# Strassen-Winograd pairs in a fused attention and GEGLU kernel: more pairs, two at a time

## The chip, the cores and the metric

One core of one Trainium2 chip runs the whole program. The metric is the device time of one launch in microseconds. A core has five engines with a queue each: PE (TensorE, matrix products, with PEld for its weight loads), DVE (VectorE), ACT (ScalarE), POOL (GpSimd) and SP, which issues transfers. PE writes only to PSUM, eight banks of 128 x 512 float32; the other engines empty those banks into SBUF, except POOL, which works on SBUF alone here.

## The reference

```
q' = exp(q - max) / sum over the head's 64 columns
k' = exp(k - max) / sum over the 576 rows
x  = q' @ (k'^T @ v)              # per batch (8) and head (8); heads side by side: 4608 x 512
h  = gelu(x @ w_gate) * (x @ w_val)   # 512 -> 1536, twice
out = h @ w_out                       # 1536 -> 512, float32
```

## The kernel before

**Blocks.** The 576 rows of a batch are cut into 512 main rows and 64 remaining ones. The main rows of batch b are block b (0 to 7). The remaining rows of all eight batches, 8 x 64 = 512, are gathered in `xtr` and make block 8. The order is 0, 1, ..., 6, 8, 7. Every block goes through two parts: the *gate/value part* makes `ht`, 12 chunks of 128 rows of h (transposed: 128 hidden columns by 512 rows of x), and the *output part* multiplies it by w_out.

**The direct way.** For one chunk and one of gate and value, four matmuls of 128x128 by 128x512 (one per 128 columns of x). ACT takes the gelu of the gate bank to SBUF, DVE multiplies it with the value bank and writes `ht`. Each such half-chunk is a call of `half`.

**Pairs.** From block 3 on, some chunks are made two at a time by the Strassen-Winograd scheme: chunks k and k+3 with both halves of the 512 rows form a 2x2 block product that takes seven products of half size instead of eight (`product_gv`, L572). A pair has four steps in `fi_pairs`: products 1 and 5 (with an ACT copy of bank pa to pb, L623, and a snapshot of pc, L608); 6 and 3; 7 and 2; 4. It holds three banks, pa, pb and pc. The results for the upper 256 rows are assembled by DVE in a float32 tile `cc` (L612), go through a gelu on ACT (L639), and are multiplied to `ht` by POOL (L640). The lower 256 rows come from pb and pa by an ACT gelu and a DVE product (L601, L602). The scheme needs sums of weight blocks, made once by `sum_wgv` on DVE, and four sums of x per block, made by `sum_x` on POOL (L570) from the finished `xt`. In blocks 3 to 8, six of the twelve chunks are pairs (k = 0, 1, 2) and six are direct.

**Output.** From block 1 on, `out_strassen` (L668) does the same with h: seven products of twelve 128x256 matmuls, accumulated in banks a, b and c, with snapshots `sn` (L690) and additions `yo` (L696) on DVE between them. It needs sums of h blocks: `sum_h` (L552) makes `sh` on DVE and, for most columns, the other two on POOL. A snapshot of a bank must be finished before the next product adds to that bank.

**What sets the order.** Everything is written out by hand: each engine executes its instructions in the order in which the Python code emits them. Small jobs for the attention of later batches are hung on points of that order by `at(b, kind, i, ...)` and emitted by `ride(b, kind, i)`. They are: loads, `exp` on ACT, the norm of q (`norm_sum` on DVE, `norm_mul` on POOL), the transposing transfer `unit_td`, the cast of v on POOL (`cast_v`), the k'^T v product `unit_kv4` and the x product `unit_x4`. Banks are handed out by `big`: the tag that was free longest goes next, and a held bank returns at `let_go`.

Of the kernel before, what the change touches and what calls it, by code (L numbers as in the profile page):

```python
# [18 lines left out]
def kernel(  # L19
# [86 lines left out]
    for i in range(2):  # L106
# [6 lines left out]
    ws = {nm: const.tile([P, 3, 2, NO // 2 * P], f16, name=f"ws{nm}") for nm in "gv"}  # L113
    xs = const.tile([P, 4, 2, 256], f16)
    q0r = const.tile([64, H, D], f32)
    eq0r = const.tile([P, C], f16)
    ld_b = {nm: [const.tile([P, H, NC * D], f32, name=f"{nm}t{i}") for i in range(n)]
            for nm, n in (("k", 2), ("v", 1), ("q", 1))}

# [29 lines left out]
    def load(src, nm, b, h0, h1, n0):  # L149
        tiles[(nm, b)] = ld_b[nm][b % len(ld_b[nm])]  # L150
        for t, c0 in ((0, n0), (1, 1)):
            (nc.scalar if b == 0 and t == 1 else nc.sync).dma_start(
                out=tiles[(nm, b)][t:P:2, h0:h1, c0 * D:NC * D],
                in_=src[b, h0:h1].rearrange("h (m n) d -> m h (n d)", n=NT)[
                    :, :, (4 * t + c0) * D:(4 * t + NC) * D])
# [36 lines left out]
    def exp(nm, b, h0=0, h1=H, n0=0):  # L192
        dst = ek_b[0] if nm == "k" else eq_b[b % 2]
        o, i = (("p n (c t d) -> p c t n d", "p c t (n d) -> p c t n d") if b >= QUAD else
                ("p n (h d) -> p h n d", "p h (n d) -> p h n d"))
        nc.scalar.activation(  # L196
            out=dst[:, n0:NC, h0 * D:h1 * D].rearrange(o, d=D, **({"t": 2} if b >= QUAD else {})),
            in_=heads(tiles[(nm, b)], b, h0, h1)[..., n0 * D:NC * D].rearrange(i, d=D),
            func=ACTF.Exp)
# [10 lines left out]
    def norm_sum(b, hp, n0=0):  # L210
        n = NC - n0
        e = eq_b[b % 2][:, n0:NC, hp * P:(hp + 1) * P].rearrange("p n (h d) -> p n h d", d=D)
        rq = att.tile([P, n, 2], f32, name="rq", tag="rq", bufs=4)
        nc.vector.reduce_sum(rq, e, axis=mybir.AxisListType.X)  # L214
        rrq = att.tile([P, n, 2], f32, name="rrq", tag="rrq", bufs=4)
        nc.vector.reciprocal(out=rrq, in_=rq)
        st[(b, "norm", hp)] = (e, rrq, n)

    def norm_pair(b, g, n0, engs):

        n = NC - n0
        e = eq_b[b % 2][:, n0:NC, 2 * g * P:(2 * g + 2) * P].rearrange("p n (h d) -> p n h d", d=D)
        rq = att.tile([P, n, 4], f32, name="rq2", tag="rq2", bufs=2)
        nc.vector.reduce_sum(rq, e, axis=mybir.AxisListType.X)
        rrq = att.tile([P, n, 4], f32, name="rrq2", tag="rrq2", bufs=2)
        nc.vector.reciprocal(out=rrq, in_=rq)  # L226
        for j, eng in enumerate(engs):
            st[(b, "norm", 2 * g + j)] = (e[:, :, 2 * j:2 * j + 2], rrq[:, :, 2 * j:2 * j + 2], n)
            norm_mul(b, 2 * g + j, eng)
# [9 lines left out]

    def exp_rem0():  # L240
        nc.scalar.activation(out=eq0r[0:64, :].rearrange("p (h d) -> p h d", d=D), in_=q0r,
                             func=ACTF.Exp)

    def norm_rem0():
# [5 lines left out]
        nc.vector.tensor_tensor(  # L250
# [84 lines left out]
    def unit_t(b, g, eng="dve", between=()):  # L335
# [3 lines left out]
        for j in range(2):  # L339
            hp = 2 * g + j  # L340
            for f in between if j == 1 else ():
                f()
            for n in range(NM):
                nc.tensor.transpose(
                    pst[:, j, n * P:(n + 1) * P],
                    eq_b[b % 2][:, n + 1, hp * P:(hp + 1) * P], ident)
# [3 lines left out]
    def unit_trem(b):  # L350

        src = eq0r[0:64] if b == 0 else eq_b[b % 2][:, 0, :]
# [6 lines left out]
    def unit_td(b):  # L359
# [3 lines left out]
                                    in_=eq_b[b % 2].rearrange("p n c -> p (n c)"))  # L363
# [192 lines left out]
    def sum_wgv(nm, i):  # L556
        w = wg_sb if nm == "g" else wv_sb
        n = NO // 2 * P
        a11, a21 = w[:, 0:2, 0:n], w[:, 0:2, n:2 * n]
        a12, a22 = w[:, 2:4, 0:n], w[:, 2:4, n:2 * n]  # L560
        t = [ws[nm][:, i] for i in range(3)]
# [4 lines left out]
    def sum_x(xt):  # L566
# [5 lines left out]
    def product_gv(i, ps, xt, k, first):  # L572
        lo, hi = slice(k * P, (k + 1) * P), slice((k + NO // 2) * P, (k + NO // 2 + 1) * P)
        for t, w, nm in ((0, wv_sb, "v"), (1, wg_sb, "g")):
            for c in range(2):
                a = {1: w[:, c, lo], 2: w[:, 2 + c, lo], 3: ws[nm][:, 2, c, lo], 4: w[:, 2 + c, hi],
                     5: ws[nm][:, 0, c, lo], 6: ws[nm][:, 1, c, lo], 7: w[:, c, hi]}[i]
# [5 lines left out]
    def fi_pairs(b, xt):  # L583
        cs = [(c, nm) for k in range(NO // 2) for c in (NO + k, NO + NO // 2 + k) for nm in "gv"]
        psg = {}

        def half(n):
            c, nm = cs[n]
            t = big([P, 512], f32, "ps" + nm)
            mm_gv(t, wg_sb if nm == "g" else wv_sb, xt, c, range(HP))  # L590
            if nm == "g":
                psg[c] = ffn.tile([P, 512], f32, name="gl", tag="gl")
                nc.scalar.activation(out=psg[c], in_=t, func=ACTF.Gelu)  # L593
            else:
                nc.vector.scalar_tensor_tensor(out=ht[:, c, :], in0=t, scalar=_H_SCALE,  # L595
                                               in1=psg[c], op0=ALU.mult, op1=ALU.mult)
            ride(b, HF, n)

        def final(ps, fi):
# [6 lines left out]
        def snap(ps):  # L606
            sn = ffn.tile([P, 2, 256], f32, name="snq", tag="snq", bufs=3)
# [6 lines left out]

        ride(b, HF, -1)
        half(0)
        half(1)
        for k in range(NO // 2):
            cc = ffn.tile([P, 2, 2, 256], f32, name="cc", tag="cc", bufs=1)
# [6 lines left out]
            s5 = snap(pc)  # L626
            half(3 * k + 2)
# [5 lines left out]
            half(3 * k + 3)  # L633
# [4 lines left out]
            glc = ffn.tile([P, 2, 256], f32, name="glc", tag="gl")  # L638
            nc.scalar.activation(out=glc, in_=cc[:, :, 1], func=ACTF.Gelu, scale=1.0 / _H_SCALE)  # L639
            nc.gpsimd.tensor_tensor(  # L640
                out=ht[:, k:NO:NO // 2, 256:512], in0=cc[:, :, 0], in1=glc, op=ALU.mult)
            half(3 * k + 4)
            product_gv(4, pa, xt, k, False)
            final(pa, k + NO // 2)
            if k == NO // 2 - 1:
                half(11)
            ride(b, PR, k)
# [3 lines left out]
    def product(i, ps, first, ts=(0, 1)):  # L651
        for j in range(NO):
            for t in ts:
# [5 lines left out]
                if w is None:  # L659
                    w = tw[{4: 4, 5: 1, 6: 2, 7: 3}[i]][:, j]  # L660
                nc.tensor.matmul(ps[t], a, w, start=(first and j == 0 and (  # L661
                    t == ts[0] or ps[t].tensor is not ps[ts[0]].tensor)),
                                 stop=(j == NO - 1), skip_group_check=True)
# [4 lines left out]
    def out_strassen(b, last):  # L668
# [31 lines left out]
        def second():  # L700
            get("b")
            product(2, ps["b"], True)
            add("b", s1, 0, 0)
            for x in tiles_["b"]:
                let_go(x)

        late = b == B
        get("a")
        product(1, ps["a"], True)
        s1 = snap("a")  # L710
        if not late:
            second()
        sum_h(*last_js(b), (4,))
        get("c")
        product(5, ps["c"], True)
        if not late:
            sum_h(*last_js(b), (3,))
        s5 = snap("c")
        if late:
            sum_h(*last_js(b), (3,))  # L720
        product(6, ps["a"], False)
        s2 = snap("a")
        ride(b, NS, 2)
        product(3, ps["c"], False)
        add("c", s2, 0, 1)
        for x in tiles_["c"]:
            let_go(x)
        if not late:
            store_rows(b, 0, yo[0])
# [3 lines left out]
        product(7, ps["a"], False)  # L733
        add("a", s5, 1, 1)
        ride(b, NS, 4)
        if late:
            second()
            store_rows(b, 0, yo[0])
        product(4, ps["a"], False)
# [101 lines left out]
    FI, NS, HF, PR = range(4)  # L841
# [7 lines left out]
    def load_2nd():  # L849
        load_batch(2, ((q, "q"), (k, "k")))  # L850
        for h0 in (0, 4):
            nc.sync.dma_start(out=q0r[:, h0:h0 + 4], in_=q[0, h0:h0 + 4].rearrange(
                "h (m n) d -> m h (n d)", n=NT)[:, :, 0:D])
# [42 lines left out]
    at(2, FI, NFI - 1, L(exp, "q", 4), L(exp, "k", 4), exp_rem0)  # L896
    at(3, HF, 8, L(norm_rem0))
    at(3, HF, 11, L(unit_trem, 0))
    for b in range(3, B):
        n = b + 1  # L900
        if n < B:
            at(b, HF, -1, L(norm_sum, n, 0), L(norm_mul, n, 0, "pool"), L(norm_sum, n, 1),
               L(norm_mul, n, 1, "pool"))
            at(b, HF, 1, L(norm_sum, n, 2), L(norm_mul, n, 2, "pool"))
            at(b, HF, 2, L(norm_sum, n, 3), L(norm_mul, n, 3, "pool"))
            at(b, HF, 3, L(unit_td, n))
        if n + 1 < B:
            at(b, HF, 0, L(load_2, n + 1))
            at(b, HF, 5, L(cast_v, n + 1, 0, 4))
            at(b, HF, 8, L(cast_v, n + 1, 4, 8))  # L910
            at(b, HF, 11, L(exp, "q", n + 1), L(exp, "k", n + 1))
    for b in range(2, B - 1):
        n = b + 1
        at(b, NS, 4, L(unit_x4, n, ("act", "dve"), 0 if n == 4 else None))
# [4 lines left out]
        at(b, NS, 4, L(preload, ACTF.Gelu), L(lambda n: sum_x(get_xt(n)), n) if n < B - 1 else L(sum_x, xtr))  # L919
    at(B, NS, 2, L(lambda: sum_x(get_xt(B - 1))))  # L920
    for b in range(3, B + 1):
        for j in range(NO // 2 - 1):
            at(b, PR, j, L(sum_h, j, NO, (1, 2)), L(sum_h, j, NO, (3, 4), "pool"))
# [6 lines left out]
    for b in order:  # L930
# [9 lines left out]
        if b > 2:  # L940
            fi_pairs(b, xt)
# [18 lines left out]
        else:  # L960
            sum_h(*last_js(b), (1, 2))
# [31 lines left out]
```

## Time and profile before

The median is 301.44 us (three runs, 301.3 to 301.6); the profiled execution spans 299.4 us.

| engine | busy us | share of the span |
|---|---|---|
| PE | 287.1 | 96% |
| DVE | 213.5 | 71% |
| ACT | 173.1 | 58% |
| POOL | 161.7 | 54% |

| groups that the change touches | count | mean ns |
|---|---|---|
| direct matmuls of gate, value 128x512 (L443) | 264 each | 379 |
| matmuls of pairs 128x256 (L580) | 504 | 273 |
| DVE `cc` (L612), 128x512 | 36 | 684 |
| POOL product to `ht` (L640), 128x512 | 18 | 1267 |
| POOL sums of x (L570), 128x512 | 24 | 1190 |
| POOL cast of v (L172), 128x640 | 26 | 769 |
| POOL norm of q (L233), 128x640 | 25 | 1282 |

[...]Matmuls overlap, so the price of one is the distance from its start to the next one's. The same holds, in a smaller measure, for ACT and DVE: the next instruction starts before the one ahead has ended. A share of the span is a mean over stages; a stage has to be read by itself.

### The profile page before, as it was taken

What the parts mean: (1) busy time and instruction counts of PE and PEld (TensorE: products, weight loads), DVE (VectorE), ACT (ScalarE), POOL (GpSimd) and SP (SyncE); (2) the same over time, 40 slices, a digit from 0 to 9 for tenths busy, and PEclk for the clock granted to TensorE, in tenths of its full rate; (3) what the DMA queues carried; (4) which work ended last, traced back from release to release, by engine and by line L of the source; (5) the groups of instructions that cost most, each with busy time, mean ns of one, the idle gap of its engine ahead of it and who ended that gap; (6) DMA issues with size and microseconds to landing.
All of it is one profiled execution on the core that took longest, in us unless ns stands there. A gap on an engine that the chain in (4) does not pass through costs nothing. (4 is left out here: it accounts for less than half of the span.)

```text
span 299.4 us, 5905 instructions
## 1 busy us (share of the span) xinstructions
PE 287.1 (96%) x2293; PEld 188.4 (63%) x2293; DVE 213.5 (71%) x411; ACT 173.1 (58%) x269; POOL 161.7 (54%) x149
## 2 busy tenths in 40 slices
PE   3999999999999999899999999999999999899994
PEld 1544445446744586568666876687668666676683
DVE  2953479998767889786867786878687557845762
ACT  4763467777652576558656956595652465126530
POOL 1557558870336009991599359944981536803610
PEclk9999999999999999999999999999999999999999
DMA  7999999997189106960399029802140300023003
GB/s 225 372 383 390 400 389 388 332 319 208 74 286 306 42 2 227 384 100 2 127 344 233 3 113 347 242 2 101 54 77 0 123 21 0 2 61 81 0 2 140
DMA packets 54619, 51.69 MB, mean 173 GB/s; under 512 B 18496, under 2 KB 50496, under 8 KB 54592
## 3 DMA queue, kind: packets, MB, share of 16 engines
q1 hardware_dynamic: 52864, 49.49, 52.0%
q10 hardware_dynamic: 1728, 1.84, 1.9%
q8 instruction: 18, 0.29, 0.4%
q14 instruction: 9, 0.07, 0.1%
HBM read 37.75 MB, written 9.44 MB: 158 GB/s over the span
## 5 line engine op out<-in xcount | busy, mean ns | idle before, releaser
L443 PE MATMUL psg<-xt,wg_sb 128*128 128x512 f16 x264 | 69.8, 379 | 0.0
L443 PE MATMUL psv<-xt,wv_sb 128*128 128x512 f16 x264 | 69.7, 379 | 0.0
L443 PEld LDWEIGHTS <-wv_sb 128*128 128x128 f16 x288 | 28.1, 98 | 27.4 <-issue 0.2
L233 POOL TENSOR_TENSOR eq<-eq,rrq 128x640 f16<-128x640 f16 (+1 forms) x27 | 34.5, 1297 | 19.7 <-DVE rrq L226 7.3
L443 PEld LDWEIGHTS <-wg_sb 128*128 128x128 f16 x288 | 28.1, 98 | 25.3
L661 PEld LDWEIGHTS <-ht 128*128 128x128 f16 x384 | 37.2, 98 | 7.1 <-issue 0.8
L448 ACT ACTIVATE gl<-psg 128x512 f32<-128x512 f32 x36 | 21.0, 597 | 29.0 <-PE psg L443 28.9
L640 POOL TENSOR_TENSOR ht<-cc,glc 128x512 f16<-128x512 f32 x18 | 22.8, 1267 | 24.1 <-ACT glc L639 24.1
L449 DVE SCALAR_TENSOR_TENSOR ht<-psv,gl 128x512 f16<-128x512 f32 x36 | 24.2, 684 | 16.0 <-PE psv L443 13.7
L570 POOL TENSOR_TENSOR xs<-xt 128x512 f16<-128x512 f16 x10 | 12.0, 1200 | 43.1 <-ACT xt L174 43.1
L595 DVE SCALAR_TENSOR_TENSOR ht<-psv,gl 128x512 f16<-128x512 f32 x36 | 24.6, 684 | 4.5 <-PE psv L443 2.4
L593 ACT ACTIVATE gl<-psg 128x512 f32<-128x512 f32 x36 | 21.3, 591 | 7.9 <-PE psg L443 7.8
L172 POOL CAST v<-vt 128x640 f16<-128x640 f32 x26 | 19.1, 769 | 12.0 <-PE pskv L319 10.5
L661 PE MATMUL psa<-tw,ht 128*128 128x256 f16 x192 | 23.5, 273 | 0.2 <-DVE yo L696 0.2
L214 DVE TENSOR_REDUCE rq<-eq 128x10 f32<-128x640 f16 x28 | 22.2, 793 | 1.6 <-ACT eq L196 1.6
L196 ACT ACTIVATE ek<-kt 128x1280 f16<-128x1280 f32 (+1 forms) x11 | 19.1, 1748 | 5.6 <-DMA kt<-in_k_dram 4.1
L580 PEld LDWEIGHTS <-wv_sb 128*128 128x128 f16 x144 | 14.0, 98 | 12.8 <-DVE cc L612 1.8
L661 PEld LDWEIGHTS <-sh 128*128 128x128 f16 x192 | 18.7, 98 | 3.5 <-issue 1.0
L552 POOL TENSOR_TENSOR ht<-ht 128x512 f16<-128x512 f16 x12 | 16.7, 1396 | 6.5 <-DVE sh L552 6.5
L196 ACT ACTIVATE eq<-qt 128x2560 f16<-128x2560 f32 (+2 forms) x10 | 18.4, 1863 | 2.6 <-DMA qt<-in_q_dram 2.5
L601 ACT ACTIVATE glq<-pgb 128x256 f32<-128x256 f32 x18 | 6.9, 383 | 21.6 <-PE pgb L580 21.2
L612 DVE SCALAR_TENSOR_TENSOR cc<-pgc,snq 128x512 f32<-128x512 f32 x18 | 12.4, 686 | 7.5 <-ACT snq L608 7.5
(136 smaller groups left out, 566.5 us busy)
## 6 DMA issues: line engine op xcount, KB each, us to landing
out_dram<-yo SPq DMA_DIRECT2D x15, 512.0 KB, 3.4
kt<-in_k_dram SPq DMA_DIRECT2D x7, 640.0 KB, 8.4
vt<-in_v_dram SPq DMA_DIRECT2D x7, 640.0 KB, 5.1
qt<-in_q_dram SPq DMA_DIRECT2D x7, 640.0 KB, 6.8
qt<-in_q_dram SPq DMA_DIRECT2D x8, 512.0 KB, 7.4
wost<-in_moe_w_out_dram SPq DMA_DIRECT2D x6, 512.0 KB, 7.9
kt<-in_k_dram SPq DMA_DIRECT2D x6, 512.0 KB, 9.8
vt<-in_v_dram SPq DMA_DIRECT2D x6, 512.0 KB, 5.7
```

The lines of the kernel that those rows point to most:

```text
L172: nc.gpsimd.tensor_copy(out=dst, in_=src)
L196: nc.scalar.activation(out=dst[:, n0:NC, h0 * D:h1 * D].rearrange(o, d=D, **({"t": 2} if b >= QUAD else {})), in_=heads(tiles[(nm, b)], b, ...
L214: nc.vector.reduce_sum(rq, e, axis=mybir.AxisListType.X)
L233: (nc.gpsimd if eng == "pool" else nc.vector).tensor_tensor(out=e, in0=e, in1=rrq.unsqueeze(-1).to_broadcast((P, n, 2, D)), op=ALU.mult)
L443: nc.tensor.matmul(ps, w[:, ci, fi * P:(fi + 1) * P], xt[:, ci, :], start=(ci == 0), stop=(ci == HP - 1))
L448: nc.scalar.activation(out=gl, in_=psg, func=ACTF.Gelu)
L449: nc.vector.scalar_tensor_tensor(out=ht[:, fi, :], in0=psv, scalar=_H_SCALE, in1=gl, op0=ALU.mult, op1=ALU.mult)
L552: (nc.gpsimd if eng == "pool" else nc.vector).tensor_tensor(out=o, in0=a, in1=b, op=op)
L593: nc.scalar.activation(out=psg[c], in_=t, func=ACTF.Gelu)
L595: nc.vector.scalar_tensor_tensor(out=ht[:, c, :], in0=t, scalar=_H_SCALE, in1=psg[c], op0=ALU.mult, op1=ALU.mult)
L640: nc.gpsimd.tensor_tensor(out=ht[:, k:NO:NO // 2, 256:512], in0=cc[:, :, 0], in1=glc, op=ALU.mult)
L661: nc.tensor.matmul(ps[t], a, w, start=(first and j == 0 and (t == ts[0] or ps[t].tensor is not ps[ts[0]].tensor)), stop=(j == NO - 1), ski ...
```

## The change

**More pairs.** Blocks 4 to 6 make four pairs (k = 0, 1, 2 and 6, the last being chunks 6 and 9), blocks 8 and 7 make six (k = 0, 1, 2, 6, 7, 8), so that these two have no direct chunk. The purpose is one eighth fewer matmul columns per pair. The weight sums for the new pairs are made by DVE in the output parts of blocks 3 to 6. Room for them is taken from the second k tile (`kt1`); a second `cc` and the second set of sums of x lie in the second eq tile and in the v tile, so blocks from 4 on use one buffer each of k and eq.

**Two pairs in turns.** The order of a gate/value part is now a string of steps (`THREE`, `FOUR`, `SIX`): "0.1" is step 1 of pair 0, "7g" is the gate of direct chunk 7, a bare word is a point for small jobs. Two pairs alternate, so that ACT and DVE have time between two steps of the same pair. The two alternate between two `cc` tiles, and the gelu writes into `cc` in place.

**The output takes late tiles late.** The first output product runs over chunks 0, 3, 1, 4 first; step 4 of the last pair ("2.4", or "8.4" in blocks 8 and 7) is emitted between those and the rest, with the second product in between in blocks 4 to 6. In block 8's output, step 1 of block 7's first pair stands ahead of the last product.

**Small jobs moved.** The cast of v goes from the gate/value part into the output part. The norm sums of q take two head pairs at once. The remaining rows of batch 0 are loaded, normalized and multiplied later (blocks 4 to 6 instead of 0 to 3), and their last norm product is on POOL. The sums of x for block 7 go from block 8's output to point `s0` of its gate/value part. The upper product of the very last pair of blocks 8 and 7 is made by DVE.

```diff
-    def fi_pairs(b, xt):
-        cs = [(c, nm) for k in range(NO // 2) for c in (NO + k, NO + NO // 2 + k) for nm in "gv"]
...
+    THREE = ("a 6g l 6v n 0.1 9g 0.2 9v t 0.3 7g 0.4 s0 1.1 7v 1.2 10g 1.3 10v 1.4 s1 2.1 8g 2.2"
+             " 8v 2.3 11g 2.4 11v")
+    FOUR = ("a 7g l 7v n 0.1 6.1 0.2 6.2 t 0.3 6.3 10g 0.4 6.4 s0 1.1 10v 1.2 8g 1.3 8v 1.4 s1 2.1"
+            " 11g 2.2 11v 2.3")
+    SIX = ("0.1 6.1 0.2 6.2 0.3 6.3 0.4 1.1 6.4 s0 7.1 1.2 7.2 1.3 7.3 1.4 2.1 7.4 s1 8.1 2.2 8.2"
+           " 2.3 8.3 2.4")
+    steps = {b: (THREE if b == 3 else SIX if b >= B - 1 else FOUR).split() for b in range(3, B + 1)}
...
+        def upper(cc):
+            nc.scalar.activation(out=cc[:, :, 1], in_=cc[:, :, 1], func=ACTF.Gelu,
+                                 scale=1.0 / _H_SCALE)
+            (nc.vector if k == NFI - NO // 2 - 1 else nc.gpsimd).tensor_tensor(
+                out=ht[:, k:k + NO // 2 + 1:NO // 2, 256:512], in0=cc[:, :, 0], in1=cc[:, :, 1],
+                op=ALU.mult)
...
+        js = (0, 1, 2, 3, 4, 5) if b < 3 else (0, 3, 1, 4, 2, 5)
         get("a")
-        product(1, ps["a"], True)
+        product(1, ps["a"], True, js=js[:4])
+        if b > 3:
+            pair_step(b, get_x(b), NO // 2 - 1 if b < B - 1 else NFI - NO // 2 - 1, 4)
+        ride(b, PR, "e")
+        get("b")
+        if 3 < b < B - 1:
+            product(2, ps["b"], True, js=js)
+        product(1, ps["a"], False, js=js[4:])
+        sum_h(*last_js(b), (1, 2))
         s1 = snap("a")
...
+        if b == B:
+            go_on(B - 1, get_x(B - 1), 1)
+        product(4, ps["a"], False, js=js)
...
-            at(b, HF, 5, L(cast_v, n + 1, 0, 4))
-            at(b, HF, 8, L(cast_v, n + 1, 4, 8))
-            at(b, HF, 11, L(exp, "q", n + 1), L(exp, "k", n + 1))
+            at(b, PR, "l", L(load_2, n + 1))
+            at(b, NS, 2, L(cast_v, n + 1, 0, H))
+            at(b, PR, "e", L(exp, "q", n + 1), L(exp, "k", n + 1))
...
-    at(B, NS, 2, L(lambda: sum_x(get_xt(B - 1))))
+    at(B, PR, "s0", L(lambda: sum_x(get_x(B - 1), xs_b[1])))
     for b in range(3, B + 1):
         for j in range(NO // 2 - 1):
-            at(b, PR, j, L(sum_h, j, NO, (1, 2)), L(sum_h, j, NO, (3, 4), "pool"))
+            at(b, PR, f"s{j}", L(sum_h, j, NO, (1, 2)), L(sum_h, j, NO, (3, 4), "pool"))
+    for b, i, what in ((3, 1, "g1 v1"), (3, 2, "g2 v2 g3 v3"), (3, 3, "g4 v4")):
+        for x in what.split():
+            at(b, NS, i, L(sum_wgv, x[0], int(x[1]), NO, 1))
+    for b, i, what in ((4, 2, "g1 g2"), (4, 3, "g4"), (5, 2, "v1 v2"), (6, 1, "v4"),
+                       (6, 2, "g3 v3")):
+        for x in what.split():
+            at(b, NS, i, L(sum_wgv, x[0], int(x[1]), NO + 1, 2))
```

## The prediction

> **What bounds the kernel now.** I read the table of stages first (one row per block's gate/value part and per block's output part; cut points from the timeline of TensorE), then TensorE's waits, then the chain that ended last, then one stretch of the timeline.
>
> The stages (stretch, us, then busy time of PE, PEld, DVE, ACT, POOL, granted clock, DMA share, GB/s):
>
> ```profile
> 113.87:135.51 21.64, 19.87 (x135) 12.83 (x132) 17.53 (x34) 12.78 (x27) 20.11 (x19) 1.00 0.76 222
> 135.51:146.28 10.77, 10.77 (x149) 9.18 (x148) 8.53 (x17) 8.31 (x9) 1.50 (x2) 1.00 0.13 50
> 146.28:165.85 19.57, 19.57 (x135) 12.90 (x132) 14.37 (x30) 13.01 (x27) 18.41 (x18) 1.00 0.86 242
> 165.85:176.73 10.88, 10.81 (x141) 9.04 (x140) 8.37 (x18) 8.26 (x8) 2.53 (x3) 1.00 0.13 50
> ...
> 236.55:256.08 19.53, 19.53 (x134) 12.91 (x132) 11.07 (x22) 12.55 (x25) 11.45 (x10) 1.00 0.07 29
> 256.08:266.43 10.35, 9.51 (x86) 8.13 (x85) 8.27 (x12) 0.00 (x0) 5.37 (x5) 1.00 0.01 2
> 266.43:285.96 19.53, 19.53 (x135) 12.92 (x133) 11.05 (x21) 12.54 (x25) 8.37 (x7) 1.00 0.24 55
> ```
>
> Rows 1 and 2 are block 3, rows 3 and 4 block 4, then block 8 (two rows) and block 7. TensorE is busy wall to wall in nearly all; the second number to see is POOL: 18.4 to 20.1 us of 19.6 to 21.6 in blocks 3 and 4, and almost idle in the output part behind them.
>
> TensorE's waits (us in total, times, longest):
>
> ```profile
> PE pswarm L435 <- ACT warm L787: 4.9, 1, 4.9
> PE pga L580 <- DVE cc L612: 1.8, 2, 1.4
> PE psa L661 <- DVE sn L690: 0.8, 1, 0.8
> ```
>
> Past the start TensorE waits for VectorE alone: in block 3 for `cc`, in block 8's output for `sn`. Against an unstalled 19.53, block 3 loses 2.11 us; block 8's output takes 10.35 where its seven products need 7 x 1.31 = 9.17, so it loses 1.18.
>
> Prices of TensorE, from the chain that ended last (start, us, what):
>
> ```profile
> 263.97 1.31 PE psb L661 x12
> ...
> 267.45 0.86 PE psv L443 x4
> 268.32 0.44 PE pga L580 x4
> ```
>
> Why block 8's output stalls (timeline: start, us, engine, line, what):
>
> ```profile
> 256.50 1.15 POOL L570 TENSOR_TENSOR xs<-xt 128x512 f16<-128x512 f16 x1
> 257.11 0.82 DVE L552 TENSOR_TENSOR sh<-ht 128x512 f16<-128x512 f16 x1
> ...
> 257.73 1.22 POOL L570 TENSOR_TENSOR xs<-xt,xs 128x512 f16<-128x512 f16 x1
> 257.97 1.26 DVE L552 TENSOR_TENSOR sh<-sh,ht 128x512 f16<-128x512 f16 x1
> ...
> 259.88 1.47 PE L661 MATMUL psa<-tw,sh 128*128 128x256 f16 x12 [0.84 <-DVE sn L690]
> ```
>
> The two `sh` sums take 0.82 and 1.26 here; their median over 24 each is 0.43. Each ends about 0.28 after the POOL instruction running when it began. `sn` stands behind them on VectorE.
>
> [...]
>
> **The change, part by part.**
>
> *Matmuls.* A pair replaces 16 matmuls of 512 columns (4 x 0.864 = 3.456) by 28 of 256 (7 x 0.436 = 3.052): 0.404 saved. Pairs added: one each in blocks 4, 5, 6, three each in 8 and 7, nine in all: 3.64 us, all on the path. Evacuation per pair, in start-to-start times of the trace: ScalarE 4 x 0.50 + 2 x 0.27 = 2.54 us, VectorE 2 x 0.60 + 2 x 0.35 + half a pair of sums 0.4 = 2.3, POOL 1.23 + 1.28 = 2.5. All under 3.05, so no engine is the bound by its sum; the question is order.
>
> *Block 3.* The norm of eq0r (0.67 + 0.20 + 0.71 on VectorE) leaves; it stood ahead of the second stall (0.58 of the 2.11). Joined norm sums (one reduce of 1280, extrapolated from 0.79 at 640 and 1.22 at 1024 to about 1.5, and one reciprocal) save about 0.4 before the first. Left: about 1.1. Gain 1.0. The eight small weight sums in its output (about 0.27 each, from 0.42 at 512) fit between the snapshots: walking VectorE through, each snapshot ends 0.1 to 0.3 ahead of the product that needs it. Nothing there.
>
> *Outputs of blocks 4 and 5.* Now the last products stand against the output: pair 2's step 3 ends where the output begins (call it 0). VectorE: `ht` of 11v at -0.01, `cc` to 0.68; ScalarE gelu to 1.35; POOL's product (1.27) to 2.66. The first `sh` waits for that. Four casts of v (0.69 each) stand right behind on POOL and are ready, so they start first: `sh` waits for cast one (3.3) and ends 3.6, the second waits for cast two and ends 4.5, `sn` of psa ends 5.14. Product 6 wanted it at 4.36: 0.84 lost. Then yo, two more sums behind casts three and four, `sn` of psc ends 7.1; product 3, due at 6.5, starts 7.16: 0.65 lost. Together 1.49. Lower bound, no contention: `sn` of psa 4.2, in time; `sn` of psc 6.06 against 5.67, 0.45 lost. I take 1.49, as the casts' inputs are long there. Less 0.404, less the 0.23 that block 4 lost already: +0.86 and +1.09. Block 6 casts nothing: 0.45 lost, less 0.404 and 0.16: -0.11. In the gate/value parts of 4 to 6, POOL's sums of x (to 3.77), four norm products (to 8.65), and two products (to 11.1) hold up the first `sh`, behind which `cc` of pair 1 ends at 13.84 for a product due at 13.91: no slack, counted at nothing.
>
> *Block 8.* Time 0 is its first product; step 4 of pair 2 is due at 40 x 0.436 = 17.44. POOL runs in order: products of pairs 0 and 6, 6.0 to 8.5; then the four sums of x for block 7, which now stand here (1.15 each, plus two `sh` between them: to 13.3); sums of turn 1, 2.3 (to 15.6); products of pairs 1 and 7, 2.5 (to 18.1). On VectorE the `sh` of turn 2 waits for that, and `cc` of pairs 2 and 8 stand behind it: sh 0.8, three `cc` of 0.60 to 0.69, to 20.8. TensorE's step 4 starts 20.85: 3.4 late. Earlier waits (1.3, for `cc` of pair 1 behind `sh` against the sums of x) are inside that. In exchange the output, free of those sums, loses about 0.3 in place of 1.18; 1.22 of matmuls go. Sum: +3.4 + 0.3 - 1.18 - 1.22 = +1.3.
>
> *Block 7.* Same queue, no sums of x: POOL's product of pair 7 ends at 15.1 and step 4 of pair 2 waits 0.3 to 1.1 (ScalarE's copies arrive 0.1 to 0.3 late in each turn; whether they add up I can't tell). I take 0.7: -0.52.
>
> *Hidden:* the larger weight sums of blocks 4 to 6 (0.42 each, while VectorE waits for products 3 and 7); remainder of batch 0 moved from block 3's to block 6's output (0.1 each way); its loads; sharing of eq, k and v buffers (their DMA and exp have over 3 us to spare); [...].
>
> Sum: -1.0 + 0.86 + 1.09 - 0.11 + 1.3 - 0.52 = +1.6, so 303.1.
>
> **Rivals.** (1) TensorE's work decides: no new stall but block 3's, so -3.64 - 1.0 = 296.8; with block 8's 1.18 also gone, 295.6. For it: no engine is at its limit per pair, and a 3.6 us cut on a full TensorE is real. Against: it takes POOL's two sets of x sums and casts as free where POOL is the fullest engine. (2) A draw: the casts lose against `sh` (1.04 less in blocks 4 and 5 each) or block 8's wait is half: 301.44 + 1.6 - 1.9 = 301.1. [...] (3) Worse: the slack of nothing in blocks 4 to 6 turns into 0.4 each and block 7 takes its upper end: 303.1 + 1.2 + 0.4 = 304.7.
>
> **How the numbers follow.** Forecast 0.46, rival 3 0.13, rival 2 0.20, rival 1 0.21. Slower (over 302.04): the forecast and rival 3, 0.59. Same: 0.14, from rival 2. Faster: rival 1 and a part of rival 2, 0.27. Range: at the low end blocks 4 and 5 at their lower bounds, block 7 at its best and block 8 at 2.8 late leave about -1.8: 299.6; the upper end adds 1.9 (rival 3 and a little): 305.0. Rival 1 is left out.
>
> **What would show it.** Right: in block 8's gate/value part TensorE waits about 3 us in all for VectorE's `cc` (line 643), VectorE's `sh` waits for POOL's `ht` (649), POOL is busy from 6 us to the end; the outputs of blocks 4 and 5 take about 11.5 us past step 4, with `sh` over 0.8 and TensorE waiting for `sn` (743); block 3's part near 20.6; PE's waits in all above 6 us past the start. Wrong: POOL's sums run faster than in before, `sh` near 0.43 beside the casts, or waits of TensorE below 2 us, in which case rival 1 holds.

## The result, and the profile after

The changed kernel takes 302.76 us (median of four runs, 302.72 to 302.79) against 301.46 (301.3 to 301.6) before, measured together: a ratio of 1.0043, 95% interval 1.0026 to 1.0061. It is slower by 1.3 us (the interval leaves out 1), though TensorE has 3.64 us less to do. The profiled executions span 300.9 and 299.4 us.

TensorE's longest waits in the changed kernel after the start (engine, line, waited-for engine, tile and line; us in total, times, longest):

```profile
PE pga L605 <- DVE eq L643: 2.3, 2, 1.2
PE psc L711 <- DVE sn L743: 1.5, 3, 0.5
PE psa L711 <- DVE sn L743: 1.2, 2, 0.6
PE pga L605 <- DVE cc L643: 0.6, 1, 0.6
```

Before, these rows came to 2.6 us; now they come to 5.6. Gaps of 0.05 to 0.2 between matmuls don't show in this view, so the losses below are larger than these waits. Line 643 writes `cc`; the second `cc` lies in the eq tile and so is called `eq` in half of the rows. The first row is block 8 (twice), the next two are the outputs of blocks 4, 5 and 6, the last is block 3.

The stages, with the columns of the prediction's table (stretch, us, then busy time of PE, PEld, DVE, ACT, POOL, granted clock, DMA share, GB/s): block 3's gate/value part, block 4's output, block 6's output, then both parts of blocks 8 and 7 without the last output.

```profile
113.86:134.19 20.33, 19.71 (x135) 12.84 (x133) 15.77 (x28) 12.93 (x28) 17.19 (x15) 1.00 0.79 233
...
163.53:176.07 12.54, 11.40 (x146) 9.44 (x144) 10.68 (x23) 10.24 (x12) 5.42 (x7) 1.00 0.12 45
...
226.00:237.13 11.13, 10.67 (x115) 8.94 (x113) 9.14 (x21) 2.89 (x7) 1.90 (x3) 1.00 0.12 46
237.13:258.53 21.40, 18.97 (x167) 15.88 (x164) 14.20 (x26) 15.46 (x33) 18.42 (x16) 1.00 0.07 27
258.53:269.37 10.84, 10.71 (x98) 9.39 (x96) 7.69 (x15) 2.77 (x7) 1.28 (x1) 1.00 0.11 25
269.37:287.35 17.98, 17.91 (x159) 15.19 (x156) 12.16 (x25) 14.35 (x31) 10.02 (x8) 1.00 0.20 45
```

The gate/value parts of blocks 4 to 6 take 18.69 or 18.70, full of TensorE, so the stalls are elsewhere. An output part from block 4 on now begins ahead of step 4 of the last pair, so 0.44 us of TensorE's work have moved into it from the part before; block 8's output also holds 0.87 of block 7's first step. Block by block (both parts together, that 0.87 counted to block 7), measured against the forecast in the prediction's terms:

| block | forecast | measured |
|---|---|---|
| 3 | -1.0 | -1.43 |
| 4 | +0.86 | +0.78 |
| 5 | +1.09 | +1.05 |
| 6 | -0.11 | +0.19 |
| 8 | +1.3 | +1.49 |
| 7, with the end | -0.52 | -0.57 |
| sum | +1.6 | +1.51 |

In the last row but one, 0.33 of the gain is not the change's. The last instruction of the kernel ends 10.25 us after block 7's output part begins, against 9.81 before; the moved 0.44 is all of that. What differs is the stretch from there to the end of the span: 3.3 us against 3.6. It is 3.3 also in before_pool8, which ends with the code of the kernel before, and 3.6 in no_cast, which ends with that of the changed kernel. Block 7 itself has gained 0.24, and the last instruction comes 1.83 us later than before.

Where block 4's output loses its time, on VectorE (start, us, instruction; in brackets the idle time ahead of it and who ended it):

```profile
166.26 0.91 DVE L575 TENSOR_TENSOR sh<-ht 128x512 f16<-128x512 f16 x1 [0.37 <-POOL ht L649]
167.20 0.82 DVE L575 TENSOR_TENSOR sh<-sh,ht 128x512 f16<-128x512 f16 x1
167.94 0.68 DVE L743 TENSOR_SCALAR sn<-psa 128x512 f32<-128x512 f32 x1
...
169.26 0.42 DVE L575 TENSOR_TENSOR s<-ht,sh 128x512 f16<-128x512 f16 x1
169.59 0.42 DVE L575 TENSOR_TENSOR ht<-ht 128x512 f16<-128x512 f16 x1
```

and what GpSimd does meanwhile:

```profile
164.95 1.27 POOL L649 TENSOR_TENSOR ht<-cc 128x512 f16<-128x512 f32 x1 [1.34 <-ACT cc L647]
166.17 3.10 POOL L188 CAST v<-vt 128x640 f16<-128x640 f32 x4
```

`sh` can't start before GpSimd's late product has ended. But the casts stand right behind that product, need nothing from anyone, and are under way some 0.09 us earlier than `sh`. Two sums of 0.43 become 0.91 and 0.82, and `sn`, which product 6 needs, is late by as much. The two sums after it (169.26 and 169.59) take 0.42 again: the casts end at 169.27.

Block 8, GpSimd (the sums of x for block 7 are the rows whose output is called `vt`, the tile whose room they use):

```profile
245.78 1.15 POOL L592 TENSOR_TENSOR vt<-xt 128x512 f16<-128x512 f16 x1
...
249.48 1.15 POOL L592 TENSOR_TENSOR vt<-xt,vt 128x512 f16<-128x512 f16 x1
...
254.06 1.27 POOL L649 TENSOR_TENSOR ht<-cc 128x512 f16<-128x512 f32 x1
```

and VectorE:

```profile
246.10 1.11 DVE L575 TENSOR_TENSOR sh<-ht 128x512 f16<-128x512 f16 x1
247.24 1.26 DVE L575 TENSOR_TENSOR sh<-sh,ht 128x512 f16<-128x512 f16 x1
...
255.36 0.43 DVE L575 TENSOR_TENSOR sh<-ht 128x512 f16<-128x512 f16 x1 [1.40 <-POOL ht L649]
```

The same sums are held up twice in two ways: in turn 1 beside GpSimd's sums of x (1.11 and 1.26), in turn 2 by the queue (1.40 of waiting for a product that itself stood behind the four sums of x). TensorE then waits 1.17 and 1.14 for the `cc` that stand behind `sh`.

### The profile page after: what moved, and what is told of

It reads as the page before. It is cut to its first block, busy times and chain, and to the rows that moved or that the text cites. A ratio compares the mean times of both kernels' runs of the same rounds, so it can differ in the third digit from the quotient of the medians.

```text
span 300.9 us, 6202 instructions
## 1 busy us (share of the span) xinstructions
PE 285.8 (95%) x2401; PEld 198.8 (66%) x2401; DVE 224.8 (75%) x430; ACT 187.9 (62%) x305; POOL 172.0 (57%) x157
## 5 line engine op out<-in xcount | busy, mean ns | idle before, releaser
L466 PE MATMUL psg<-xt,wg_sb 128*128 128x512 f16 x216 | 57.4, 379 | 0.0
L466 PE MATMUL psv<-xt,wv_sb 128*128 128x512 f16 x216 | 57.4, 379 | 0.0
L249 POOL TENSOR_TENSOR eq<-eq,rrq 128x640 f16<-128x640 f16 (+1 forms) x27 | 34.7, 1304 | 19.5 <-DVE rrq L242 7.2
L471 ACT ACTIVATE gl<-psg 128x512 f32<-128x512 f32 x36 | 21.0, 598 | 28.8 <-PE psg L466 28.6
L472 DVE SCALAR_TENSOR_TENSOR ht<-psv,gl 128x512 f16<-128x512 f32 x36 | 24.2, 684 | 16.0 <-PE psv L466 13.7
L466 PEld LDWEIGHTS <-wg_sb 128*128 128x128 f16 x216 | 21.0, 98 | 20.7
L649 POOL TENSOR_TENSOR ht<-eq 128x512 f16<-128x512 f32 x13 | 16.5, 1272 | 20.5 <-ACT eq L647 20.5
L605 PEld LDWEIGHTS <-wg_sb 128*128 128x128 f16 x216 | 21.1, 98 | 2.5
L659 ACT COPY pgb<-pga 128x512 f32<-128x512 f32 x27 | 15.9, 590 | 10.2 <-PE pga L605 10.0
L633 DVE SCALAR_TENSOR_TENSOR ht<-pga,glq 128x256 f16<-128x256 f32 x27 | 11.1, 422 | 13.7 <-ACT glq L632 13.7
L632 ACT ACTIVATE glq<-pgb 128x256 f32<-128x256 f32 x27 | 10.2, 378 | 15.8 <-PE pgb L605 9.5
L605 PE MATMUL pga<-xs,wv_sb 128*128 128x256 f16 x84 | 16.0, 272 | 2.9 <-DVE eq L643 2.3
```

The costliest lines, as they stand in the source:

```text
L249: (nc.gpsimd if eng == "pool" else nc.vector).tensor_tensor(out=e, in0=e, in1=rrq.unsqueeze(-1).to_broadcast((P, n, 2, D)), op=ALU.mult)
L466: nc.tensor.matmul(ps, w[:, ci, fi * P:(fi + 1) * P], xt[:, ci, :], start=(ci == 0), stop=(ci == HP - 1))
L471: nc.scalar.activation(out=gl, in_=psg, func=ACTF.Gelu)
L472: nc.vector.scalar_tensor_tensor(out=ht[:, fi, :], in0=psv, scalar=_H_SCALE, in1=gl, op0=ALU.mult, op1=ALU.mult)
L605: nc.tensor.matmul(ps[:, t], a, x, start=(first and t == 0 and c == 0), stop=(c == 1), skip_group_check=True)
L633: nc.vector.scalar_tensor_tensor(out=ht[:, fi, 0:256], in0=ps[:, 0], scalar=_H_SCALE, in1=gl, op0=ALU.mult, op1=ALU.mult)
```

## The experiments

Each ran beside the kernel before, whose median was 301.27 to 301.46 in all of them; times are medians, and the intervals are those of the ratio to it. Where nothing else is said, an experiment starts from the changed kernel.

**x7_in_out.** One part undone: the sums of x for block 7.

```diff
-    at(B, PR, "s0", L(lambda: sum_x(get_x(B - 1), xs_b[1])))
+    at(B, NS, 2, L(lambda: sum_x(get_x(B - 1), xs_b[1])))
```

> One part undone: GpSimd's four sums of x for block 7 stand in block 8's output again, as in the kernel before, and no longer after turn 0 of block 8. Theory (these sums hold up GpSimd's queue, and through it the sh and cc sums of VectorE): block 8's gate/value part, 21.4 us in the changed kernel, falls to 18.9 (17.9 without a stall, and the 1.0 that block 7 loses in the same order of turns); its output loses about 0.9 more to the sums of x; in all 302.8 - 2.5 + 0.9 = 301.2. Rival (two pairs in turns are by themselves too much for ScalarE's copies): the gate/value part stays above 20.5, and the time rises to 303.5.

Measured: 302.69 us, ratio 1.0047 (1.0032 to 1.0062). Block 8's gate/value part fell from 21.40 to 19.12, as the theory had it; its output rose from 10.84 to 12.97, by 2.1 and not 0.9. VectorE in that output:

```profile
258.93 1.03 DVE L575 TENSOR_TENSOR sh<-ht 128x512 f16<-128x512 f16 x1
260.00 1.26 DVE L575 TENSOR_TENSOR sh<-sh,ht 128x512 f16<-128x512 f16 x1
...
262.55 1.10 DVE L575 TENSOR_TENSOR s<-ht,sh 128x512 f16<-128x512 f16 x1
```

So the queue account of the gate/value part holds, and the rival (turns as such) falls; but the sums of x cost about the same in either place, because in both they run beside VectorE's sums. The move itself was worth nothing.

**x_swap.** The sums of x for block 8 on VectorE, those for block 7 on GpSimd at the same time.

```diff
...
-        at(b, NS, 4, L(lambda n: sum_x(get_x(n)), n if n < B - 1 else B))
+        if n < B - 1:
+            at(b, NS, 4, L(lambda n: sum_x(get_x(n)), n))
+        else:
+            at(b, NS, 4, L(lambda: sum_x(xtr, eng="dve")),
+               L(lambda: sum_x(get_x(B - 1), xs_b[1])))
...
-    at(B, PR, "s0", L(lambda: sum_x(get_x(B - 1), xs_b[1])))
```

> The sums of x for block 8 go to VectorE (0.42 each, while it is idle at the start of block 8) and those for block 7 to GpSimd at the same place, where it now does those of block 8; nothing stands after turn 0. Theory: block 8's gate/value part 18.9, its output as in the changed kernel: 302.8 - 2.5 = 300.3. Should the two sets of sums hold each other up, the first sums of block 8 come up to 1.2 us later and the part takes 19.5 to 20. Rival (the turns themselves are the bound): above 20.5.

Measured: 302.16 us, ratio 1.0029 (1.0018 to 1.0040). Block 8's part: 20.66, 0.7 less than in the changed kernel and not 2.5. The stalls of turns 1 and 2 are gone, but the sums at the head hold each other up. VectorE:

```profile
237.73 0.74 DVE L592 TENSOR_TENSOR xs<-xtr 128x512 f16<-128x512 f16 x1
238.51 1.25 DVE L592 TENSOR_TENSOR xs<-xtr,xs 128x512 f16<-128x512 f16 x1
239.68 1.37 DVE L592 TENSOR_TENSOR xs<-xtr 128x512 f16<-128x512 f16 x1
```

Sums that take 0.42 alone take up to 1.37, and TensorE loses 0.87 at the first product of sums and 0.86 at the first `cc`. The number is a miss: 20.66 is above the 19.5 to 20 named for this case, and by itself it would fall to the rival (above 20.5). The trace decides against the rival: of the 2.8 lost against 17.88, the sums make 1.7, and the turns only the short gaps that they have in every version. It is a third view of the same hold-up.

**no_cast.** The casts of v left out.

```diff
-            at(b, NS, 2, L(cast_v, n + 1, 0, H))
+            if n + 1 not in (6, 7):
+                at(b, NS, 2, L(cast_v, n + 1, 0, H))
```

> The casts of v for blocks 6 and 7 (in the outputs of blocks 4 and 5) are left out, so blocks 6 and 7 are computed with an old v. Theory [...]: the sh sums take 0.43 in place of 0.8 to 0.9, product 6 is in time, product 3 is 0.45 late in place of 0.69; 1.0 less in each of the two outputs, 300.8 in all. Rival (the upper product of pair 2, which ends late on GpSimd, is the whole cause): both outputs keep their two stalls, 302.8.

Measured: 301.41 us, ratio 0.9995 (0.9980 to 1.0010). `sh` takes 0.42, product 6 is in time, and both outputs fall from 12.54 and 12.53 to 11.66. Product 3 is still 0.58 late, not 0.45. So of the 1.46 that each output loses, the casts make 0.88. The other 0.58 is not the casts': VectorE works without a pause through the snapshot that product 6 needs, `yo`, two sums of 0.42 and the snapshot that product 3 needs. The two snapshots start 1.99 us apart, TensorE's product between them takes 1.31, and VectorE begins late, behind GpSimd's late product. The total fell by 1.3, not by the 2.0 expected or the 1.8 of the two outputs; the profile has 0.3 of the difference in the 3.6 behind its last instruction.

**sums_pool.** Two sums moved between the engines, so that GpSimd's queue itself keeps the casts back.

```diff
-        sum_h(*last_js(b), (4,))
+        sum_h(*last_js(b), (4,), "pool" if 3 < b < B - 1 else "dve")
...
-        sum_h(*last_js(b), (3,))
+        sum_h(*last_js(b), (3,), "pool" if 3 < b < B - 1 else "dve")
```

> In the outputs of blocks 4 to 6 the last third of sums 4 and 3 goes to GpSimd, ahead of the casts of v in its queue; they wait for VectorE's sh, so no cast can stand in front of sh. Theory: both stalls go, in blocks 4 and 5 (1.46 each) and the 0.59 of block 6; casts end about 3.3 us later, just as the k-v products want v (bound: 0 to 0.6 lost there in each of blocks 4 and 5). 302.8 - 3.5 = 299.3, up to 300.5. Rival (the wait only moves, to the sums on GpSimd at 1.15 in place of 0.42, or to the casts): 302 or more.

Measured: 299.40 us, ratio 0.9936 (0.9919 to 0.9953), as the theory had it. The outputs of blocks 4, 5 and 6 take 11.08, 11.11 and 10.55, with no wait of TensorE for `sn` left anywhere. GpSimd in block 4's output:

```profile
167.39 1.16 POOL L575 TENSOR_TENSOR s<-ht,sh 128x512 f16<-128x512 f16 x1 [1.00 <-DVE sh L575]
168.51 1.15 POOL L575 TENSOR_TENSOR ht<-ht 128x512 f16<-128x512 f16 x1
169.62 3.37 POOL L188 CAST v<-vt 128x640 f16<-128x640 f32 x4
```

GpSimd now waits for `sh` (1.00), and everything behind it in the queue waits too. The sums cost 1.15 there in place of 0.42, but products 3 and 7 want them later than that; VectorE is free of two sums ahead of its snapshots, and the 1.99 between their starts becomes 1.33. So the edit does two things at once: it keeps the casts back, and it shortens VectorE's walk from snapshot to snapshot. Block 6 casts nothing, and its output still gains 0.58, by the second alone.

**casts_gv.** The casts where the kernel before had them.

```diff
-    FOUR = (... 10g 0.4 6.4 s0 1.1 10v 1.2 8g 1.3 8v 1.4 s1 2.1"
+    FOUR = (... 10g 0.4 6.4 s0 1.1 10v c0 1.2 8g 1.3 8v c1 1.4 s1 2.1"
...
-            at(b, NS, 2, L(cast_v, n + 1, 0, H))
+            (at(b, NS, 2, L(cast_v, n + 1, 0, H)) if b == 3 else
+             (at(b, PR, "c0", L(cast_v, n + 1, 0, 4)), at(b, PR, "c1", L(cast_v, n + 1, 4, 8))))
```

> The changed kernel with the casts of v of blocks 6 and 7 back in the gate/value parts of blocks 4 and 5 (two halves, about where the kernel before had them). Theory (GpSimd is full there: 17.1 us of an 18.7 us part, with the casts 19.9): its products and the sums behind them come later, sh and cc with them, and the gate/value parts take 19.5 to 20.2, the outputs 11.5: about 302.8 + 2 x (1.1 - 1.0) = 303.0, within 1. Rival (GpSimd has room): the parts stay at 18.7 and the outputs lose nothing or 0.6: 300.8 or less.

Measured: 302.67 us, ratio 1.0047 (1.0032 to 1.0062). The total is near what the theory gave, by another way, so it can't be claimed: the gate/value part stays at 18.70 although GpSimd works 18.08 of it, and the output takes 12.46, with 0.60 lost at step 4 of the last pair (`cc` behind two sums `sh` of 0.91 and 0.82, again beside a cast) and 0.68 at product 3. The casts cost this output 0.88 in the changed kernel and 0.80 here (12.46 against 11.66 in no_cast); in both VectorE's sums run beside them or behind their queue, and GpSimd's full count is not the reason.

**three.** One pair fewer in blocks 4 to 6.

```diff
-... if b == 3 else SIX if b >= B - 1 else FOUR).split()
+    THREE_B = ("a 6g l 6v n 0.1 9g 0.2 9v t 0.3 7g 0.4 s0 7v 1.1 10g 1.2 10v 8g 1.3 8v 1.4 s1"
+               " 2.1 11g 2.2 11v 2.3")
+... if b == 3 else SIX if b >= B - 1 else THREE_B).split()
```

In it the plain products of chunk 9 read weights that a weight sum has already replaced in place, so that one of the twelve hidden chunks is other numbers; the amount of work is not touched by that.

> The changed kernel with three pairs in place of four in blocks 4 to 6 (pair 6, four quarters of hidden columns, goes back to plain products), the rest and the end of each part as they are. Theory (TensorE sets the pace of these parts, a pair saves 0.404): each part 18.7 + 0.4 = 19.1, the outputs unchanged, 302.8 + 1.2 = 304.0. Rival (GpSimd, VectorE or ScalarE sets the pace): no change or a shorter part, 302.8 or less.

Measured: 304.26 us, ratio 1.0097 (1.0082 to 1.0113). The gate/value parts take 19.09, 19.10 and 19.09 against 18.69, 18.70 and 18.70: 0.40 each, the price of a pair. The total rose by 1.5, of which these are 1.2. In these parts TensorE does set the pace, and the saving arrives in full.

**pool8.** The cure of the outputs extended to block 8, with block 7's sums of x behind it.

```diff
-        sum_h(*last_js(b), (4,))
+        sum_h(*last_js(b), (4,), "pool" if b > 3 and b != B - 1 else "dve")
...
-        sum_h(*last_js(b), (3,))
+        sum_h(*last_js(b), (3,), "pool" if b > 3 and b != B - 1 else "dve")
...
-    at(B, PR, "s0", L(lambda: sum_x(get_x(B - 1), xs_b[1])))
+    at(B, NS, 2, L(lambda: sum_x(get_x(B - 1), xs_b[1])))
```

> Block 7's sums of x stand in block 8's output, and the last thirds of sums 4 and 3 go to GpSimd in the outputs of blocks 4, 5, 6 and 8, so that in all four they are in its queue ahead of the casts of v and of the sums of x. Theory [...]: block 8's gate/value part 19.1 as with the sums in the output before, and its output 10.5 in place of the 13.0 it took there; 299.4 - 2.3 - 0.3 = 296.8. Rival (GpSimd's sums of x come too late for block 7, or its 1.15 us sums too late for product 3): output of block 8 above 11.5, 298 or more.

Measured: 296.80 us, ratio 0.9853 (0.9837 to 0.9869): as expected, and faster than both kernels. Block 8's two parts and block 7's first in this version:

```profile
233.76:252.87 19.11, 18.98 (x167) 15.89 (x165) 12.76 (x27) 15.44 (x33) 14.01 (x12) 1.00 0.08 32
252.87:263.42 10.55, 10.55 (x99) 9.39 (x97) 7.07 (x13) 2.77 (x7) 8.03 (x7) 1.00 0.11 25
263.42:281.38 17.96, 17.90 (x159) 15.12 (x157) 12.16 (x25) 14.33 (x31) 10.02 (x8) 1.00 0.20 45
```

The sums of x are the same four instructions in the same output as in x7_in_out; behind two sums that wait for `sh`, they cost TensorE nothing: 10.55 against 12.97 there, and against 10.84 in the changed kernel, where no sums of x stand in this output.

**pool8_copy.** On top of pool8, an attempt on the rest of what blocks 8 and 7 lose.

```diff
-            nc.scalar.copy(out=pb, in_=pa)
+            copy_on("dve" if b >= B - 1 and k >= NO else "act", pb, pa)
```

> On top of the version before this one, the copy of psum tile pga to pgb of pairs 6 to 8 in blocks 8 and 7 goes from ScalarE to VectorE, which is idle there for 0.86. Theory (the last 1.0 to 1.2 that each of the two gate/value parts loses are gaps of 0.2, 0.1 and 0.2 in each of two turns, which begin with ScalarE's copy of the second pair ending late): block 8 18.2, block 7 17.1 us; 296.8 - 1.9 = 294.9. Rival (VectorE's own queue is as late): no change or worse, 296.8 or more.

Measured: 301.03 us, ratio 0.9991 (0.9983 to 1.0000); a clear miss, the rival's side. VectorE's idle 0.86 was there, but the copy is not in it:

```profile
243.17 0.42 DVE L575 TENSOR_TENSOR sh<-sh,ht 128x512 f16<-128x512 f16 x1
243.51 0.69 DVE L192 COPY pgb<-pga 128x512 f32<-128x512 f32 x1
```

The copy is emitted after `sh` and starts when `sh` is through, about 2 us after its input was there; product 6 of the second pair waits 1.33 to 1.39 for it, four times. The small gaps behind it (0.1 and 0.2 in each turn) are gone, which fits the account that ScalarE's copies start them, but no run removes the first gap, so this stays likely and not shown.

**before_pool8.** The same cure in the kernel before, alone.

```diff
-        sum_h(*last_js(b), (4,))
+        sum_h(*last_js(b), (4,), "pool" if b == B else "dve")
...
-            sum_h(*last_js(b), (3,))
+            sum_h(*last_js(b), (3,), "pool")
```

> The kernel before, with nothing of the change but one cure: in block 8's output the last thirds of sums 4 and 3 go to GpSimd, ahead of the sums of x for block 7 in its queue. Theory [...]: sh sums at 0.43, output 9.2 to 9.3 in place of 10.35, 301.4 - 1.1 = 300.3. The best changed version (296.8) would then be 3.5 below a kernel with the same cure, against the 3.64 counted for nine pairs and about 1.4 more saved in block 3, less the 2.2 that blocks 8 and 7 lose in their turns. Rival (the sh sums are slow for another reason): no change, 301.4.

Measured: 299.85 us, ratio 0.9956 (0.9940 to 0.9973). Block 8's output takes 9.17, the seven products and nothing else: the 1.18 was `sh` beside the sums of x (0.82 and 1.26 in the kernel before) and what follows from it. Here the two moved sums stood behind the late snapshot in VectorE's queue, so that it is not their leaving that helps. The total is 0.45 below the 300.3 expected; the profile has most of that behind the last instruction (3.3 us in place of 3.6). With this cure on both sides the changed kernel leads by 3.05 us, not the 3.5 expected.

**pool8_v3.** On top of pool8, a weight sum of block 2 moved out of block 3's head.

```diff
-            at(b, NS, 4, L(sum_wgv, "v", 4), L(sum_wgv, "v", 3), one_ring)
+            at(b, NS, 1, L(sum_wgv, "v", 3))
+            at(b, NS, 4, L(sum_wgv, "v", 4), one_ring)
```

Here weight sum 1 of v, which comes later, reads a weight block that number 3 has already replaced, and number 2 is built on number 1, so the v side of the pairs is other numbers.

> On the version at 296.8: one weight sum of block 2 (v, number 3, 1.50 us on VectorE at the head of block 3, beside GpSimd's sums of x) is done in the output of block 2 behind the snapshot of psc, where VectorE is idle for 0.56 and GpSimd too. Theory [...]: the sum takes 0.55, the wait goes, block 3's gate/value part 19.5: 296.8 - 0.8 = 296.0. Rival (the joined norm sums, 1.47 each, make cc late): 0.3 or more of the wait stays, 296.4 or more.

Measured: 296.05 us, ratio 0.9828 (0.9813 to 0.9842). Block 3's part: 19.61, from 20.32 in pool8; the wait for `cc` is gone. In the changed kernel the sum stood at the head of this part:

```profile
114.33 1.50 DVE L586 TENSOR_TENSOR wv_sb<-wv_sb 128x768 f16<-128x768 f16 x1
```

Its new place leaves it at 0.55. The joined norm sums, 1.47 each, stayed where they were, so that rival falls.

**pool8_v13.** As pool8_v3, with the order of the sums kept.

```diff
-    at(2, NS, 2, L(sum_wgv, "v", 1), L(sum_wgv, "v", 2))
+    at(2, NS, 1, L(sum_wgv, "v", 1))
+    at(2, NS, 2, L(sum_wgv, "v", 2), L(sum_wgv, "v", 3))
...
-            at(b, NS, 1, L(sum_wgv, "v", 3))
```

> As the version at 296.05, with weight sum 1 of v moved too, so that it still comes ahead of number 3: sum 1 behind the snapshot of psc in block 2's output, sums 2 and 3 where 1 and 2 stood. VectorE is idle there for 0.56, and sums 2 and 3 take the room of 1 and 2. Theory: 296.05 again, block 3's part 19.6. Rival (sum 1 ahead of the snapshot of psa delays product 3 of block 2): 0.1 to 0.5 lost in block 2's output, 296.2 to 296.5.

Measured: 296.07 us (295.97 to 296.09), ratio 0.9822 (0.9808 to 0.9835). It is the fastest version: 5.4 us below the kernel before, 6.7 below the changed one. The view of TensorE's waits over its whole run has one row left, the start; the short gaps in the turns of blocks 8 and 7, 2.2 us in all, are still there and too short for it:

```profile
PE pswarm L458 <- ACT warm L841: 4.9, 1, 4.9
```

## Why the prediction was right

The forecast was 303.1 and the time is 302.76; most of its terms hold by their mechanism too, with some sizes off; in blocks 4 and 5 and in block 7 a part of the agreement is luck.

*Matmuls.* Held. A pair is worth 0.404 by the sum and 0.40 by the experiment with three pairs. It is saved in full; the stalls outweigh it.

*Block 3.* The gain was larger, 1.43 and not 1.0. The mis-sized term is "Left: about 1.1": the stall left is 0.78. What makes it was not among the terms at all: a weight sum of 768 columns beside GpSimd's sums of x, 1.50 in place of 0.55 to 0.58, in the kernel before as in the changed one; without it there the part takes 19.6.

*Outputs of blocks 4 and 5.* Held in sum: 1.49 forecast, 1.46 measured (0.77 at product 6 for the 0.84, 0.69 at product 3 for the 0.65). The first stall is by the cause named, `sh` beside the casts (0.91 and 0.82). The second is not behind "casts three and four": the two further sums run at 0.42, and without any cast 0.58 of it stays, where the lower bound had 0.45. It is VectorE's walk from snapshot to snapshot, which the prediction's own times add up to but which it didn't name as the cause; so here the number is right in part by luck.

*Block 6.* The mis-sized term is that same 0.45, here measured as 0.59; with 0.1 of batch 0's remainder it makes most of the step from -0.11 to +0.19.

*Block 8.* Right: 3.4 late forecast, 3.52 measured (21.40 against 41 groups of 0.436, 17.88), by the two waits named, `sh` beside the sums of x in turn 1 (1.11 and 1.26) and the queue in turn 2 (1.40). Its exchange was right as arithmetic (the output loses 0.36 and not 1.18) and wrong as a reading: in the new order the sums of x would have cost the output 2.5, not 1.18, so moving them neither won nor lost.

*Block 7.* 0.98 lost (17.98 against 17.00), in place of the 0.7 taken and inside the 0.3 to 1.1. It comes as three gaps of 0.1 to 0.2 in each turn, so the lags do add up. The path named first, GpSimd's product of pair 7, is not what is waited for: that product ends at 283.54, `sh` follows VectorE's own work at 283.82, and the first `cc` behind it waits for ScalarE:

```profile
284.98 0.69 DVE L643 SCALAR_TENSOR_TENSOR eq<-pgc,snq 128x512 f32<-128x512 f32 x1 [0.28 <-ACT snq L639]
```

Step 4 of pair 2 starts 0.18 late. Block 7 so gains 0.24 and not 0.52; that the row reads -0.57 is the shorter stretch behind the last instruction, which is luck.

*Hidden.* The weight sums of blocks 4 to 6, the loads and the shared buffers show no wait of TensorE, as forecast, and the gate/value parts of these blocks stay full with the slack counted at nothing.

*Its signs and its range.* TensorE's waits past the start come to 5.8 us and not above 6, those for `cc` in block 8 to 2.3 and not about 3; the rest of the loss is in the short gaps. The terms named for the low end of the range add up to -1.5 and not -1.8; nothing else depends on it.

The rivals: TensorE's work decides (296.8) failed not for want of the saving but by the order in GpSimd's queue and by two sums too many in VectorE's. With both mended the kernel takes 296.8, the rival's number by luck, through a sum it didn't have: 1.18 more is won in block 8's output, 0.4 more in block 3, 0.4 that the outputs of blocks 4 and 6 had lost before and 0.3 behind the last instruction, and 2.2 lost in the turns of blocks 8 and 7. The draw needed the casts to start behind `sh`, which they don't: they start 0.09 ahead of it.

That GpSimd's instructions and VectorE's sums hold each other up is measured in five kernels here (the kernel before, the changed one, x7_in_out, x_swap and casts_gv): a sum of two SBUF tiles of 128x512 takes 0.41 to 0.43 alone and 0.74 to 1.37 where it begins under a GpSimd instruction that has 0.4 or more to run. Which begins first matters: eleven sums of the changed kernel began 0.04 or 0.05 ahead of GpSimd's next sum of h; they took 0.42 or 0.43, and GpSimd's 1.39 or 1.40 in place of 1.15. The first weight sum of block 2, of 768 columns, takes 0.84 under the casts of v, against 0.55 alone. What in the chip makes them slow each other, no run shows. The `tensor_reduce` of the norms was not held up: all eight of 1280 columns take 1.47 or 1.48, at whatever point of GpSimd's sums of x or norm products they begin.

## What to carry to other kernels

When two engines hold each other up, as here (a sum of 0.42 took up to 1.37), their busy times do not say what a move costs; what mattered here is which instruction was ready first beside which (casts 0.09 ahead of `sh` made 0.91 and 0.82 of two sums of 0.43). Background work on the one engine belongs behind something in its own queue that waits for the other engine's urgent instruction: two sums moved that way in each of three outputs, dearer by 0.7 each, were worth 3.4 us. About half of it is the casts kept back (0.88 in each of two outputs); the other half came because the sums no longer stand ahead of VectorE's snapshots. And an idle gap was of no use to what is emitted behind the instruction that ends it: in pool8_copy VectorE's gap of 0.86 ended at 242.38, and the copy, emitted behind `sh`, started at 243.51.

## What the runs showed of the hardware

The hold-up goes both ways: in the kernel with both sets of sums at block 8's head, GpSimd's sums took up to 1.33 in place of 1.15 while VectorE's took up to 1.37 in place of 0.42, so the short instruction paid most there. In x7_in_out the order was the other way round at one point: VectorE's fp32 product had begun 0.2 us before GpSimd's first sum of x, and that sum took 1.60. VectorE's instructions with PSUM as one input took no longer beside GpSimd in the changed kernel: in block 4's output `sn` takes 0.68 and `yo` 0.69, both beside the casts and after them. VectorE's product of two fp32 inputs from SBUF took 0.81 there in block 8's output; it began while a product of GpSimd had 0.26 to run, so what it takes alone stays open.
